# A new order of steps for a linear-attention and gated-convolution kernel, with the last norm factor spread through DRAM

## The chip, the cores and the metric

The kernel runs on one core of one Trainium2 chip. The metric is the device time of one execution in microseconds; the smaller, the better. Times of single steps come from one profiled execution of the kernel before, and are microseconds from the start of its span.

## The reference

Eight batches, each of 576 positions and eight heads of 64. For each head, `kv` is the sum over positions of the outer products of keys and values; the queries times `kv` are normalised by their root mean square over the 64 columns and scaled by `g_norm`. The heads side by side are the 512 columns of `x` of a gated feed-forward layer with a depthwise convolution over three positions in its gate.

```python
kv = np.einsum('bhsd,bhse->bhde', k, v)
out = np.einsum('bhsd,bhde->bhse', q, kv)
rms = np.sqrt(np.mean(out * out, axis=-1, keepdims=True) + 1e-06)
x = (out / rms * g_norm)                 # (B, S, H * D) after a transpose
...
h = np.maximum(x @ w_in, 0.0)            # (B, S, 1024)
conv_out = sum of conv_w[k] * h shifted by k - 1, for k in 0, 1, 2
gate = 1.0 / (1.0 + np.exp(-conv_out))
return (h * gate @ w_out)                # (B, S, 512), float32
```

## The kernel before, in words

The kernel is a list of steps, `ORDER`, run from left to right. Each token is a step: its name, its arguments (most begin with the batch, `b`), and after `@` the buffer that it writes: a PSUM bank for steps of TensorE, a slot of a ring in SBUF for the others. At the end the program chains the instructions of every engine in the order of the list, so each engine does its own steps in exactly this order. A step waits for the steps that make its inputs, and for the last readers of the bank or slot that it takes over.

The steps, by engine:

- Loads on GpSimd's queue: `Lq`, `Lk`, `Lv` (a batch's queries, keys and values, cast to bf16), `Li`, `Lo` (the weights).
- TensorE: `fi` (matmuls of zeros at the start), `qt` (transposes of q), `kv` and `kz` (keys by values), `ot` and `ox` (queries by `kv`), `on` and `oq` (sums of squares, as a product with ones: `on` by full 128x128 matmuls, `oq` by 64x64 ones), `ss` (the same for two batches at once in a compact form, 8 rows in each group of 32), `sp` (the compact norm factor spread over 64 partitions a head, by a matmul with a 0/1 matrix), `hk`, `hs`, `hm` (a 128-column tile of `x @ w_in`; in two parts, for half the positions, for all of them), `cv` (the convolution by matmuls, for four tiles of batch 0), `om` (a 128-row tile of the output; `om.p.m.0.4` and `om.p.m.4.4` are its first and second half over the 1024 columns of `h`), `oh` (a tile in two halves of columns).
- VectorE: `qd`, `kvd`, `ed`, `dh` (evictions of q's transposes, of `kv`, of an output tile, of half of one), `mo` and `mu` (`x`, as output times `g_norm` times factor, one `scalar_tensor_tensor`), `sl` (the compact factor split into three bf16 parts, four instructions), `ta` (the two outer taps of the convolution for one tile of `h`, two instructions), `aa` and `ab` (their sum, then the middle tap), `mg` (`h` times the gate).
- ScalarE: `qa`, `kva`, `ea`, `eh` (the same evictions), `sq` (squares), `oc` (the output copied to fp32), `nl` and `ln` (the factor by a reciprocal square root), `rp`, `rh`, `re` (relu), `sg` and `sc` (sigmoid). A change between root and sigmoid loads a table.
- SP's queue: `st` and `sh` (stores of output rows), `tq` (q transposed by DMA, batches 6 and 7), `kx` (`kv` with its halves of partitions exchanged).

Batches go in pairs that share a buffer `h`. Batches 0 to 3 take the norm factor directly (`on` or `oq`, `nl`, `mo`). Batches 4 and 5, and 6 and 7, take it compactly: `sq` and `oc` of all parts, then `ss`, one `ln` for the pair, `sl`, and for each part (two of heads, `u`, by two of positions, `s`) an `sp` into two banks and a `mu` that reads it from there. `ln.6`, `sl.6`, `sp.6.*`, `sp.7.*`, `mu.6.*` and `mu.7.*` are the last pair's. In batches 6 and 7 a part has 320 positions (`s` = 0) or 256.

The two steps at the centre of the change are these:

```python
@op
def sp(b, u, s, b0):
    ps = T["sp", b, u, s] = bank2()[:, :, :width(b, s)]
    ...
        nc.tensor.matmul(ps[:, tt, :], spread[rows, ...], T["w", b0][rows, :width(b, s)], ...)
@op
def mu(b, u, s):
    nc.vector.scalar_tensor_tensor(
        x_part(b, u, s), T["o32", b, u, s], g_sb, T["sp", b, u, s], op0=AL.mult, op1=AL.mult)
```

The lines of the profile that matter here: L732 `om`, L757 `oh`, L628 `hs`, L658 `hk`, L613 `hm`, L593 `sp`, L566 `ss`, L599 `mu`, L556 `mo`, L581 to L584 `sl`, L681 and L682 `ta`, L687 `aa`, L692 `ab`, L722 `mg`, L743 `ed`, L738 `ea`, L698 `sg`, L640 `rh`, L545 `nl`, L574 `ln`, L416 `kva`, L414 `kvd`, L227 the load of a table, L748 `st`.

Of the kernel before, what the change touches and what calls it, by code (L numbers as in the profile page):

```python
# [54 lines left out]
AL = mybir.AluOpType  # L55
# [4 lines left out]
pre@0,1 af cad.q.0.0@0 cad.v.0.0@0 fi.10.512@0 qt.0.0.0@2 qd.0.0.0@0 gt.k.1.0 Li.0.4 fi.9.512@0 ct@0 Lq.1.0.2@1  # L60
Lk.1.0.2@0 Lv.1.0.2@1 Li.4.4 ps pg fi.4.512@1 cad.k.1.0@1 caa.v.1.0 caa.k.0.0 kv.0.0.1@4 kva.0.0.1@0 ot.0.0.0@6 pc
cad.v.3.0 cad.k.2.0 fi.2.512@0 cad.k.3.0 caa.q.1.0 qt.0.1.0@2 qd.0.1.0@1 sq.0.0.0@0 oq.0.0.0@4 fi.2.512@0 dg.1
caa.v.2.0 kv.0.1.1@0 fi.2.512@2 nl.0.0.0@0 kva.0.1.1 ot.0.1.0@4 sq.0.1.0@1 cad.q.0.1 qt.0.0.1@2 qa.0.0.1 fi.2.512@0
oq.0.1.0@0 nl.0.1.0@1 mo.0.0.0@0 cad.q.1.1 qt.0.1.1@6 qd.0.1.1 mo.0.1.0 ot.0.0.1@2 sq.0.0.1@2 ot.0.1.1@6 fi.1.512@0
sq.0.1.1@3 oq.0.0.1@0 nl.0.0.1@2 fi.1.512@4 fi.1.512@4 hk.0.1.0.0@4 hk.0.1.0.1 rp.1.0@0 on.0.1.1@0 nl.0.1.1@3
hk.0.2.0.0@5 hk.0.2.0.1 rp.2.0 dg.3 mo.0.0.1 dg.2 hk.0.3.0.0@4 hk.0.3.0.1 hk.0.0.0.0@2 hk.0.0.0.1 rp.0.0 hk.0.0.1.0@3
rp.3.0 hk.0.1.1.0@5 hk.0.3.1.0@0 mo.0.1.1 hk.0.3.1.1 rp.3.1 hk.0.1.1.1 rp.1.1 hk.0.0.1.1 rp.0.1 dg.0 hk.0.2.1.0@1
hk.0.2.1.1 qt.1.0.0@6 kv.1.0.1@4 rp.2.1 cv.0.2@2 sc.0.2@0 cv.0.3@0 qd.1.0.0@2 kvd.1.0.1@1 ot.1.0.1@6 sc.0.3 pl
sq.1.0.1@4 cv.0.1@4 cv.0.0@2 Lq.1.2.2 Lk.1.2.2 Lv.1.2.2 sc.0.1@1 fi.2.512@0 qt.1.1.0@0 qd.1.1.0@3 mg.0.1.1 Lo.0.8
sc.0.0 mg.0.1.0 oq.1.0.1@4 nl.1.0.1@4 mo.1.0.1@1 fi.1.512@2 hk.0.5.1.0@2 hk.0.5.0.0@3 hk.0.5.0.1 rp.5.0 hk.0.5.1.1  # L70
rp.5.1 ta.0.1.5@0 hk.0.4.1.0@0 hk.0.4.1.1 rp.4.1 hk.0.7.0.0@1 hk.0.7.0.1 kv.1.1.1@4 kvd.1.1.1 rp.7.0 ot.1.0.0@2
sq.1.0.0@5 hk.0.7.1.0@6 hk.0.7.1.1 rp.7.1 ta.0.1.7@1 ot.1.1.1@0 sq.1.1.1@6 oq.1.0.0@4 nl.1.0.0@5 mo.1.0.0 hk.0.4.0.0@6
hk.0.4.0.1 rp.4.0 hk.0.6.1.0@7 hk.0.6.1.1 rp.6.1 oq.1.1.1@4 nl.1.1.1@6 mo.1.1.1 hk.0.6.0.0@6 Lq.2.0.4@2 hk.0.6.0.1
rp.6.0 ta.0.1.4 hk.1.6.1.0@7 ta.0.1.6 hk.1.0.1.0@2 ot.1.1.0@4 sq.1.1.0@7 aa.0.1.2 hk.1.1.1.0@3 hk.1.2.1.0@6 hk.1.6.1.1
rh.1.6.1 hk.1.1.1.1 rh.1.1.1 on.1.1.0@0 nl.1.1.0@7 mo.1.1.0 hk.1.2.1.1 hk.1.5.1.0@7 hk.1.5.1.1 rh.1.5.1 rh.1.2.1
hk.1.3.1.0@3 hk.1.3.1.1 rh.1.3.1 hk.1.0.1.1 rh.1.0.1 ab.0.1.2 sg.0.1.5 sg.0.1.4 qt.2.1.0@0 qt.2.0.0@6 hk.1.5.0.0@3
hk.1.5.0.1 rh.1.5.0 qd.2.0.0@4 hk.1.0.0.0@2 hk.1.4.1.0@4 hk.1.4.1.1 hk.1.0.0.1 hk.1.1.0.0@5 hk.1.6.0.0@6 hk.1.1.0.1
hk.1.2.0.0@7 hk.1.2.0.1 rh.1.2.0 rh.1.1.0 rh.1.0.0 hk.1.6.0.1 rh.1.6.0 aa.0.1.3 qd.2.1.0@0 ab.0.1.3 sg.0.1.7 sg.0.1.6
hk.1.7.0.0@0 mg.0.1.2 hk.1.7.1.0@1 hk.1.7.1.1 rh.1.7.1 hk.1.7.0.1 rh.1.7.0 ta.1.1.1@0 ta.1.1.0 Lk.2.0.4@1 Lv.2.0.4@0
Lq.3.0.4@0 Lk.3.0.4@0 Lv.3.0.4@1 Lq.4.0.4@1 aa.1.1.0 hk.1.4.0.0@3 om.0.1.0.4@2 rh.1.4.1 hk.1.4.0.1 rh.1.4.0  # L80
om.0.2.0.4@5 kv.2.0.2@6 mg.0.1.3 om.0.1.4.4 ab.1.1.0 sg.1.1.0 sg.1.1.1 kvd.2.0.2@2 ot.2.0.1@0 sq.2.0.1@0 ed.0.1@0
st.0.1 qt.3.1.0@6 qd.3.1.0@1 Lk.4.0.4@1 Lv.4.0.4@0 Lq.5.0.4@2 om.0.2.4.4 on.2.0.1@2 qt.3.0.0@6 qd.3.0.0@2 nl.2.0.1@8
mo.2.0.1@2 om.0.3.0.4@4 ea.0.2@1 ot.2.1.1@6 ot.2.1.0@2 mg.1.1.0 om.0.3.4.4 ed.0.3@2 sq.2.1.0@1 sq.2.1.1@2 on.2.1.0@0
nl.2.1.0@9 mo.2.1.0 om.0.0.0.4@5 hk.1.3.0.0@4 on.2.1.1@0 st.0.2 nl.2.1.1@0 mo.2.1.1 om.0.0.4.4 ed.0.0@3 ot.2.0.0@2
# [54 lines left out]
def kernel(  # L139
# [685 lines left out]
```

## Time and profile before

| | us |
|---|---|
| timed, median of 3 runs (lowest to highest) | 177.59 (177.56 to 177.61) |
| profiled execution: its span | 175.6 |
| TensorE busy | 167.9 |
| VectorE busy | 149.5 |
| ScalarE busy | 148.9 |
| GpSimd busy | 22.2 |

For the profiled execution only the span, from the first to the last instruction, is given; the timed runs are others, and their median is 1.99 us longer than this span. A row of the groups reads: line, engine, operation, what is written from what, shapes, count, then the busy time in us and the mean of one in ns, then the idle time of the engine just ahead of them and what ended it. A row of the chain or of a timeline begins with its start and its length in us. The granted TensorE clock is 1.00 in every stretch.

### The profile page before, as it was taken

How to read it: one execution, taken by the hardware profiler on the slowest of the kernel's cores; microseconds unless marked ns; L12 is line 12 of the kernel's file. 1: busy time of each engine (PE TensorE's matmuls, PEld its weight loads, DVE VectorE, ACT ScalarE, POOL GpSimd, SP SyncE). 2: the span in 40 equal slices, each digit the busy share in tenths (PEclk: the TensorE clock that was granted, in tenths of full speed). 3: DMA queues.
4: the chain of work that ended last, by engine and by line, in shares of the span. 5: the costliest groups of instructions: out<-in, count | busy, mean ns of one | idle time of the engine just before them, and what ended most of it. 6: DMA issues, size and time to landing. Idle time of an engine off the chain costs nothing.

```text
span 175.6 us, 5070 instructions
## 1 busy us (share of the span) xinstructions
PE 167.9 (96%) x2097; PEld 100.0 (57%) x2114; DVE 149.5 (85%) x290; ACT 148.9 (85%) x268; POOL 22.2 (13%) x35
## 2 busy tenths in 40 slices
PE   7979999999999999999999999999999999999992
PEld 2334766676447677644467764444877744444451
DVE  2796638899688899999999998989999999999950
ACT  2368899999978999999999998999999967676721
POOL 3094512200603013030000000000000000000000
PEclk9999999999999999999999999999999999999999
DMA  5999999999999999999999050330310003064486
GB/s 159 392 323 207 207 207 207 208 208 209 207 241 230 227 207 207 170 182 197 258 181 161 14 134 0 119 123 0 119 63 0 0 0 116 13 239 175 179 304 237
DMA packets 25911, 29.11 MB, mean 166 GB/s; under 512 B 6036, under 2 KB 20384, under 8 KB 25888
## 3 DMA queue, kind: packets, MB, share of 16 engines
q0 software_dynamic: 13296, 14.50, 49.2%
q1 hardware_dynamic: 12048, 13.11, 26.2%
q10 hardware_dynamic: 544, 1.18, 1.7%
q8 instruction: 16, 0.26, 0.6%
q14 instruction: 7, 0.06, 0.1%
HBM read 32.52 MB, written 9.44 MB: 239 GB/s over the span
## 4 chain that ended last, share of the span: by engine, by line
PE 76%; DVE 12%; ACT 5%; DMA 3%; issue 3%; ACTq 0%; DVEq 0%
PE banks L732 32%; PE banks L628 14%; PE banks L613 9%; PE banks L658 4%; DMA stg<-in_v_dram 3%; PE banks L460 3%; DVE h L722 2%; PE banks L708 2%; ACT taps L698 2%; PE banks L402 2%; PE banks L593 2%; PE banks L433 1%; PE banks L528 1%; DVE taps L681 1%; PE banks L286 1%
## 5 line engine op out<-in xcount | busy, mean ns | idle before, releaser
L732 PE MATMUL banks<-w_out_sb,h 128*128 128x512 bf16 x267 | 62.8, 379 | 1.2 <-issue 0.6
L698 ACT ACTIVATE taps<-taps,cw 128x576 bf16<-128x576 bf16 (+1 forms) x44 | 40.6, 958 | 5.7 <-DVE taps L692 5.5
L732 PEld LDWEIGHTS <-h 128*128 128x128 bf16 x280 | 26.2, 98 | 30.0 <-issue 1.1
L628 PE MATMUL banks<-x,w_in_sb 128*128 128x288 bf16 (+2 forms) x256 | 34.2, 286 | 0.0
L640 ACT ACTIVATE h<-banks 128x288 bf16<-128x288 f32 (+2 forms) x80 | 29.5, 460 | 0.3 <-PE banks L658 0.2
L628 PEld LDWEIGHTS <-w_in_sb 128*128 128x128 bf16 x256 | 24.4, 98 | 7.8 <-issue 0.8
L722 DVE TENSOR_TENSOR h<-h,taps 128x1152 bf16<-128x1152 bf16 (+1 forms) x24 | 22.8, 952 | 1.2 <-ACT taps L698 1.2
L687 DVE TENSOR_TENSOR taps<-taps 128x1152 bf16<-128x1152 bf16 (+1 forms) x22 | 21.5, 978 | 0.5
L509 ACT ACTIVATE sq<-banks 128x576 bf16<-128x576 f32 (+2 forms) x32 | 20.8, 691 | 1.1 <-PE banks L460 1.1
L692 DVE TENSOR_TENSOR taps<-taps,h 128x1152 bf16<-128x1152 bf16 (+1 forms) x22 | 21.4, 972 | 0.3
L681 DVE TENSOR_SCALAR taps<-h,cw 128x576 bf16<-128x576 bf16 (+1 forms) x44 | 18.7, 424 | 0.6 <-ACT h L665 0.5
L682 DVE TENSOR_SCALAR taps<-h,cw 128x576 bf16<-128x576 bf16 (+1 forms) x44 | 18.4, 418 | 0.0
L738 ACT ACTIVATE row<-banks 128x512 f32<-128x512 f32 x23 | 13.5, 597 | 5.7 <-PE banks L732 4.2
L658 PE MATMUL banks<-x,w_in_sb 128*128 128x288 bf16 (+2 forms) x128 | 17.7, 286 | 0.1
L613 PE MATMUL banks<-x,w_in_sb 128*128 128x288 bf16 x128 | 16.9, 286 | 0.0
L556 DVE SCALAR_TENSOR_TENSOR x<-banks,cw,rs 128x576 bf16<-128x576 f32 (+2 forms) x16 | 13.0, 816 | 3.9 <-ACT rs L545 3.6
L658 PEld LDWEIGHTS <-w_in_sb 128*128 128x128 bf16 x128 | 12.0, 98 | 4.4 <-issue 0.5
L227 ACT ACT_TABLE_LOAD x10 | 12.8, 1283 | 2.0 <-issue 1.8
L613 PEld LDWEIGHTS <-w_in_sb 128*128 128x128 bf16 x128 | 12.3, 98 | 3.7 <-issue 0.2
L443 DVE COPY qT<-banks 128x1152 bf16<-128x1152 bf16 (+2 forms) x13 | 8.8, 681 | 5.7 <-PE banks L433 5.7
L545 ACT ACTIVATE rs<-banks,eps_sb 128x576 f32<-128x576 f32 (+2 forms) x16 | 11.8, 740 | 1.1 <-PE banks L528 1.1
L599 DVE SCALAR_TENSOR_TENSOR x<-o,cw,banks 128x576 bf16<-128x576 f32 (+2 forms) x16 | 12.1, 810 | 0.7 <-PE banks L593 0.5
(89 smaller groups left out, 162.9 us busy)
## 6 DMA issues: line engine op xcount, KB each, us to landing
out_dram<-row SPq DMA_DIRECT2D x35, 256.0 KB, 2.3
q_sb<-in_q_dram POOLq DMA_DIRECT2D x6, 576.0 KB, 17.9
k_sb<-in_k_dram POOLq DMA_DIRECT2D x6, 576.0 KB, 14.5
v_sb<-in_v_dram POOLq DMA_DIRECT2D x6, 576.0 KB, 17.9
stg<-in_v_dram ACTq DMA_DIRECT2D x2, 576.0 KB, 6.2
stg<-in_k_dram SPq DMA_DIRECT2D x4, 288.0 KB, 6.9
w_in_sb<-in_moe_w_in_dram POOLq DMA_DIRECT2D x2, 512.0 KB, 9.9
w_out_sb<-in_moe_w_out_dram POOLq DMA_DIRECT2D x1, 1024.0 KB, 15.5
```

The lines of the kernel that those rows point to most:

```text
L509: nc.scalar.activation(T["sq", b, u, s], T["o", b, u, s], AX.Square)
L613: nc.tensor.matmul(ps[:, s, :HS], w_in_sb[:, t, f * P:(f + 1) * P], T["x", b][:, t, c0:c1], start=(t == 0), stop=(t == NT - 1))
L628: nc.tensor.matmul(ps, w_in_sb[:, t, f * P:(f + 1) * P], T["x", b][:, t, c0:c1], start=(t == 0), stop=(t == NT - 1))
L640: nc.scalar.activation(h, fr, AX.Relu)
L658: nc.tensor.matmul(T[at], w_in_sb[:, t, f * P:(f + 1) * P], T["x", b][:, t, c0:c1], start=(t == 0), stop=(t == NT - 1))
L681: nc.vector.tensor_scalar_mul(tap[:, 0, f % 2, :n, 8:8 + S], h[:, f], cw[:, f:f + 1])
L682: nc.vector.tensor_scalar_mul(tap[:, 1, f % 2, :n, :S], h[:, f], cw[:, 2 * NF + f:2 * NF + f + 1])
L687: nc.vector.tensor_add(tap[:, 1, :, :n, :S], tap[:, 0, :, :n, 7:7 + S], tap[:, 1, :, :n, 1:1 + S])
L692: nc.vector.tensor_add(y, y, span(b, n)[:, 2 * j:2 * j + 2])
L698: nc.scalar.activation(y, y, AX.Sigmoid, scale=cw[:, NF + f:NF + f + 1])
L722: nc.vector.tensor_mul(h, h, tap_of(b, j)[:, 1, :, :n, :S])
L732: nc.tensor.matmul(T["om", p, m], h[:, f, m * P:(m + 1) * P], w_out_sb[:, f, :], start=(f == 0), stop=(f == NF - 1))
```

## The change

1. The whole list is new. Nearly all steps are the same and stand in another order, with other banks and slots. Their numbers differ as follows: `kvd.2`, `kvd.3` become `kva` (ScalarE); `ea.0.4`, `ea.1.0`, `ea.1.2`, `ea.1.4`, `ea.1.8` become `ed` (VectorE); `ed.2.8`, `ed.3.2`, `ed.3.7` become `ea`; `eh.3.8.0` becomes `dh`; `oq.1.0.0` and `oq.1.1.1` become `on`, and `on.2.0.1` becomes `oq`.
2. For batches 6 and 7, `sl.6` and the eight `sp` go. In their place `dw.6` stores the compact factor, 128 x 320 in fp32, to DRAM by SP's queue, and eight `df` fetch it for one part each, by two DMAs of SP's queue, each of which spreads one row over 64 partitions. The fetched tiles lie in slots of the rings of q, k and v, which are free by then. `mu` then reads its factor from SBUF.
3. Some steps are written more generally (`pair` gives one bank for a narrow `on`), and steps that this list does not use are added (`ff`, `ad`).

The new steps, and the changes that the list uses:

```diff
+    dram = pool("dram", 1, space=bass.MemoryType.DRAM)
...
+    def pair(n):
+        if 2 * n <= 512:
+            return bank()[:, :2 * n].rearrange("p (e n) -> p e n", e=2)
+        return bank2()[:, :, :n]
...
     def on(b, u, s):
-        ps = T["on", b, u, s] = bank2()[:, :, :c1 - c0]
+        ps = T["on", b, u, s] = pair(c1 - c0)
...
+    def dw(b0):
+        T["rd", b0] = dram.tile([P, GW], FP32, name="rd")
+        nc.sync.dma_start(out=T["rd", b0], in_=T["rs", b0])
+
+    @op
+    def df(b, u, s, b0):
+        w, c = width(b, s), 2 * (b - b0) + s
+        to = T["sp", b, u, s] = ring("qkv"[(4 * (b - b0) + 2 * u + s) % 3], [P, 2, 320], FP32, "spread")[:, :, :w]
+        fr = T["rd", b0].rearrange("(t c i) w -> c i t w", t=NT, i=2)[c, :, 2 * u:2 * u + 2, :w]
+        for i in range(2):
+            nc.sync.dma_start(out=to[half(i)], in_=fr[i].unsqueeze(0).to_broadcast([D, 2, w]))
```

The list around the last pair's factor, as it was:

```text
... ox.7.0.0@0 oc.7.0.0@8 ox.6.0.1@6 ... mg.2.2.3 om.1.6.4.4 om.1.0.4.4 ...
om.1.1.0.4@4 om.1.1.4.4 ss.6.6.2@5 ss.7.6.2 ln.6@0 ... om.1.4.0.4@0 om.1.4.4.4 ... om.1.7.4.4 ...
sl.6@1 sp.6.1.1.6@6 mu.6.1.1@0 sp.6.0.1.6@4 mu.6.0.1 sp.7.0.0.6@2 mu.7.0.0@2 ... om.1.5.0.4@0 om.1.5.4.4
sp.7.1.0.6@6 mu.7.1.0 sp.7.0.1.6@4 sp.7.1.1.6@2 om.1.3.0.4@1 om.1.3.4.4 ... hs.7.6.0@6 rh.7.6.0@1 mu.7.1.1 mu.7.0.1
...
sp.6.0.0.6@2 mu.6.0.0 sp.6.1.0.6@4 mu.6.1.0 ... aa.4.2.1 ab.4.2.1 ... sg.4.2.2 ... sg.4.2.3 ...
```

and as it is:

```text
... ox.7.0.0@0 ox.6.0.1@2 ... mg.2.2.3 om.1.0.4.4 om.1.6.4.4 kx.7@1 ta.4.2.5@1 ed.1.0@0 ta.4.2.4 ox.7.1.0@0 ta.4.2.6
ox.7.1.1@2 ox.7.0.1@4 om.1.2.4.4 ea.1.6@1 om.1.8.0.4@7 om.1.8.4.4 ed.1.2@2 aa.4.2.2 ... ed.1.8@3 ss.6.6.2@4 sq.7.1.1@6
sq.7.1.0@7 ss.7.6.2 ln.6@0 om.1.4.0.4@5 om.1.4.4.4 ab.4.2.2 aa.4.2.3 sg.4.2.4 hm.4.0@6 om.1.1.0.4@4 om.1.1.4.4
sg.4.2.5 ed.1.4@4 om.1.7.0.4@5 st.1.0 st.1.2 om.1.7.4.4 oc.7.1.1@6 re.4.0 oc.7.1.0@7 st.1.6 dw.6 st.1.8 ab.4.2.3
df.7.0.0.6@0 om.1.5.0.4@2 om.1.5.4.4 mg.4.2.2 om.1.3.0.4@0 om.1.3.4.4 sg.4.2.7 ta.4.2.1@1 ea.1.1@0 ta.4.2.0 ea.1.7@1
aa.4.2.0 mu.7.0.0@0 ea.1.5@2 df.7.1.0.6@0 hm.4.3@2 sg.4.2.6 mu.7.1.0 ea.1.3@3 ab.4.2.0 st.1.4 df.6.1.1.6@1 hs.7.6.0@0
hs.7.4.0@1 hs.7.7.0@4 hs.7.5.0@5 mu.6.1.1@1 re.4.3 df.6.0.1.6@1 mu.6.0.1 mg.4.2.3 rh.7.6.0@1 sg.4.2.1 sg.4.2.0
rh.7.7.0 df.6.0.0.6@2 hm.4.2@2 ... df.6.1.0.6@0 hs.6.0.1@4 ... st.1.1 st.1.5 st.1.7 hs.6.6.1@1 df.7.0.1.6@1 st.1.3
rh.7.2.0 df.7.1.1.6@0 mu.7.0.1 aa.4.2.1 mu.7.1.1 ab.4.2.1 rh.6.6.1 mg.4.2.0 hs.7.2.1@0 rh.7.2.1 hs.7.1.0@2 sg.4.2.3
sg.4.2.2 hs.6.3.0@1 rh.6.3.0 ... hs.7.3.0@1 hs.7.3.1@0 ...
```

Ahead of the table load of batch 1's last sigmoids the old list has `nl.3.1.0@5 ... rh.3.6.1 ... sg.1.1.5 sg.1.1.4 ... mg.1.1.2`, the new one `nl.3.1.0@1 ... sg.1.1.4 ... sg.1.1.5 ...`, with `rh.3.6.1` and `mg.1.1.2` behind them.

More of the change, by code (lines that the diff above doesn't have):

```diff
@@ L65 @@
[L65 to L74, printed above, removed]
@@ L80 @@
[L80 to L84, printed above, removed]
@@ L286, in fi, with ff @@
             nc.tensor.matmul(ps[:, :w], zero[:, :P], zero[:, :w], start=True, stop=True)
+    @op
+    def ff(n, w):
+        ps, z = bank(), zero.bitcast(FP32)
+        for _ in range(n):
+            nc.tensor.matmul(ps[:, :w], z[:, :P], z[:, :w], start=True, stop=True)
     @op
@@ L408, in kvc @@
     def kvc(eng, b, u0, n):
-        if u0 == 0:
+        if ("kvb", b) not in T:
             T["kvb", b] = ring("kvb", [P, 2, 2 * D], BF16, "kvb")
@@ L437, in qc @@
     def qc(eng, b, u, s):
-        if s == 0:
+        if ("qT", b, u) not in T:
             T["qT", b, u] = ring("qT", [P, 2, S], BF16, "qT")
@@ L532, in oq @@
         c0, c1 = cols(b, s)
-        ps = T["on", b, u, s] = bank2()[:, :, :c1 - c0]
+        ps = T["on", b, u, s] = pair(c1 - c0)
         for tt in range(2):
@@ L689, in ab, with ad, y_of @@
     @op
+    def ad(b, n, j):
+        tap = tap_of(b, j)
+        T["y", b, j] = tap[:, 0, :, :n, 7:7 + S]
+        nc.gpsimd.dma_start(out=T["y", b, j], in_=tap[:, 1, :, :n, 1:1 + S], accum_op=AL.add)
+    def y_of(b, n, j):
+        if ("y", b, j) not in T:
+            T["y", b, j] = tap_of(b, j)[:, 1, :, :n, :S]
+        return T["y", b, j]
+    @op
     def ab(b, n, j):
-        y = tap_of(b, j)[:, 1, :, :n, :S]
+        y = y_of(b, n, j)
         nc.vector.tensor_add(y, y, span(b, n)[:, 2 * j:2 * j + 2])
```

149 lines of the change are left out of this document (87 added, 62 removed).

## The prediction

> **What bounds the kernel now.** I read the page first, then the busy time by stretch of 5 us, then the chain of work that ended last, then the rows of single steps. The page's first part:
>
> ```profile
> span 175.6 us, 5070 instructions
> PE 167.9 (96%) x2097; PEld 100.0 (57%) x2114; DVE 149.5 (85%) x290; ACT 148.9 (85%) x268; POOL 22.2 (13%) x35
> ```
>
> TensorE looks like the bound, but the two 85% are averages over a thin start and a thin end. By stretch (span, then PE, PEld, DVE, ACT, POOL, granted clock, DMA share, GB/s):
>
> ```profile
> 50.00:55.00 5.00, 5.00 (x109) 2.91 (x108) 3.46 (x6) 3.56 (x8) 1.48 (x2) 1.00 1.18 240
> 95.00:100.00 5.00, 5.00 (x114) 3.98 (x113) 4.97 (x7) 5.00 (x9) 0.00 (x0) 1.00 0.35 97
> 105.00:110.00 5.00, 4.84 (x33) 2.41 (x32) 4.29 (x8) 4.51 (x8) 0.00 (x0) 1.00 0.00 0
> ```
>
> Up to 60 us VectorE and ScalarE have idle time; around 100 us all three engines are full. VectorE alone, from `mg.1.1.2` to the end of the last `mg`:
>
> ```profile
> 66.51:166.65 100.14, 96.74 (x156) 1.00 0.54 115
> ```
>
> And all that it waited for in that stretch (us in total, times, longest):
>
> ```profile
> DVE h L722 <- ACT taps L698: 1.2, 3, 0.7
> DVE x L599 <- PE banks L593: 0.5, 1, 0.5
> DVE hi L581 <- ACT rs L574: 0.3, 1, 0.3
> DVE kvb L414 <- PE banks L479: 0.2, 1, 0.2
> ```
>
> So VectorE is busy 96.74 of 100.14 us. Of the 2.2 us of waits some 0.2 ended with the first `mg` itself, and only 2.0 lie inside; the other 1.4 are short bubbles between dependent steps. TensorE and VectorE are bounds of nearly the same height, and a step taken from one alone buys little. The chain, at the places that the change touches (start, length, what):
>
> ```profile
> 62.80 0.63 ACT rs L545
> 63.43 0.30 ACT h L640
> 63.74 1.28 ACT L227
> 65.04 1.45 ACT taps L698 x2
> 66.51 0.76 DVE h L722
> ...
> 118.22 0.34 PE banks L593 x4
> ...
> 120.86 0.28 PE banks L593 x2
> 121.15 1.83 PE banks L732 x8
> ...
> 129.74 0.25 PE banks L593 x4
> 129.98 11.11 PE banks L628 x88
> ...
> 141.35 10.74 PE banks L732 x49
> 152.15 10.74 PE banks L732 x49
> 162.94 7.50 PE banks L732 x34
> 170.44 1.76 PE banks L757 x16
> ```
>
> From 121 us to the end, 170.44 + 1.76 = 172.2, TensorE works without a gap; the rest of the span is the last eviction and its store. The span is 175.6 and the timed median 177.59, so 2.0 us lie around the span; I keep these 2.0 and the 3.4 behind TensorE's end, and forecast the shift of TensorE's end.
>
> **What TensorE gets.** The eight `sp` of batches 6 and 7 go (L593, 16 matmuls). Their place is 118.22 to 121.15, 2.93 us, in which one output tile of 8 matmuls ran too (1.83 in the row at 121.15), so 1.10 us are spread and waiting for it; the third group is 0.25. In all 1.35 us. Nothing is added on TensorE: `fi`, `hs`, `hm`, `om` keep their numbers, and in batches 1 and 2 two `oq` become `on` and one `on` an `oq`, short groups far ahead of the place that I find to decide; I cost them at nothing. If TensorE were the only bound, the end would move by −1.35.
>
> **What VectorE gets.** The rows (mean ns stand ahead of the last bar):
>
> ```profile
> L743 DVE COPY row<-banks 128x512 f32<-128x512 f32 x12 | 8.2, 687 | 1.6 <-PE banks L732 1.6
> L599 DVE SCALAR_TENSOR_TENSOR x<-o,cw,banks 128x640 bf16<-128x640 f32 x4 | 3.4, 877 | 0.0
> L599 DVE SCALAR_TENSOR_TENSOR x<-o,cw,banks 128x512 bf16<-128x512 f32 x4 | 2.8, 744 | 0.5 <-PE banks L593 0.5
> L582 DVE SCALAR_TENSOR_TENSOR rs<-hi,na,rs 128x320 f32<-128x320 bf16 x2 | 1.1, 552 | 0.1
> L581 DVE CAST hi<-rs 128x320 bf16<-128x320 f32 x2 | 0.7, 328 | 0.4 <-ACT rs L574 0.3
> ```
>
> And three evictions in a row, from the timeline (start, length):
>
> ```profile
> 166.57 2.00 DVE L743 COPY row<-banks 128x512 f32<-128x512 f32 x3
> ```
>
> `sl.6` goes: two casts and two products, 2 x 0.328 + 2 x 0.552 = 1.76 us. But the new list gives evictions of output rows to VectorE just here: `ed.0.4`, `ed.1.0`, `ed.1.2`, `ed.1.4`, `ed.1.8` were `ea` on ScalarE. Three in a row took 2.00, so five cost 3.3 us. The three that VectorE loses (`ed.2.8`, `ed.3.2`, `ed.3.7`) lie behind the place that I find to decide. The two `kvd` that become `kva` lie ahead of it, where VectorE waits anyway.
>
> The eight `mu` now read the factor from SBUF rather than from a bank. No row shows this very operation. The nearest are the same instruction with one operand in a bank, (877 − 744) / 128 = 1.04 ns an element and so 744 − 532 = 212 ns fixed, and with all in SBUF (L582), 552 − 333 = 219 ns fixed. I take no difference; a fixed part as low as that of the copy from a bank (687 − 532 = 155 ns) would save 0.06 each. [...]
>
> **The fetch.** `dw.6` stores the 128x320 factor to DRAM and each `df` fetches it with two DMAs, all on SP's queue:
>
> ```profile
> out_dram<-row SPq DMA_DIRECT2D x35, 256.0 KB, 2.3
> stq<-in_q_dram SPq DMA_DIRECT2D x2, 320.0 KB, 6.5
> ```
>
> Three issues on SP, from the timeline:
>
> ```profile
> 170.33 1.30 SPq L748 DMA_DIRECT2D out_dram<-row  x3
> ```
>
> A store of 256 KB lands 2.3 us after its issue, and an issue takes 1.30 / 3 = 0.43. The fetch sends the 160 KB of one `dw` and some 164 KB per DMA. From `ln.6` to the second fetched tile: 2.3 for `dw`, three issues, 2.3 for the last DMA, 5.9 us. In the list TensorE has five output tiles (5 x 1.83 = 9.2 us) and two `hm` between `ss.7.6.2` and the first `hs` of batch 7, and VectorE eight other steps ahead of `mu.7.0.0`. The loads are over by then (the stretch at 105 us has a DMA share of 0.00). So I cost the fetch at nothing. The upper bound is the landing time in a full queue, 6.5: then 6.5 + 1.3 + 6.5 = 14.3 plus half a microsecond of `ln`, against 9.2 and two `hm` of 8 matmuls at 11.11 / 88, 11.2 together: 3.6 late. The sixteen fetches hold SP for 16 x 0.43 = 6.9 us, and `st.1.4`, `st.1.1`, `st.1.5`, `st.1.7`, `st.1.3` stand among or behind them; their row buffers are asked for again only by pair 2's evictions some 20 us later.
>
> **The sum.** The new list has a place that the old one had not. `hs.7.3.0@1` needs the bank that `rh.6.3.0` empties, and `rh.6.3.0` stands on ScalarE behind `sg.4.2.3` and `sg.4.2.2`, which wait for VectorE's `ab.4.2.1`. The rows for it, of before, from the timelines of VectorE and ScalarE and from the groups:
>
> ```profile
> 135.03 1.36 DVE L692 TENSOR_TENSOR taps<-taps,h 128x2304 bf16<-128x2304 bf16 x1
> ```
>
> ```profile
> 137.03 2.42 ACT L698 ACTIVATE taps<-taps,cw 128x1152 bf16<-128x1152 bf16 x2
> ```
>
> ```profile
> L640 ACT ACTIVATE h<-banks 128x320 bf16<-128x320 f32 x16 | 7.2, 504 | 0.0
> ```
>
> The 135.03 is `ab.4.2.1`, ending at 136.4. VectorE's work from 66.51 up to it is the same in both lists but for the terms above. Its start moves by −0.3, as the relu at 63.43 no longer stands ahead of the table load; the two `kva` fall into ScalarE's idle 1.4 us of the stretch at 50. Then −1.76 for `sl.6`, +3.3 for five `ed`, and −2.0 if every wait of the stretch goes (the third, for `sp`, goes with it, and the five `ed` fill the others). 136.4 − 0.3 − 1.8 + 3.3 − 2.0 = 135.6. Two sigmoids, 2.4, a relu, 0.5, and 0.1 between engines: `hs.7.3.0` starts at 138.6. Behind it the new list still has 34 halves of output tiles, 6 `hs` and 2 `oh`. The old one ran the same 34 from 141.1 to 170.4, 29.3 us; 24 matmuls at 11.11 / 88 are 3.0; the `oh` 1.8. TensorE ends at 172.7, 0.5 later than the 172.2 of before, though it had 1.35 less to do: without the wait it would stand at `hs.7.3.0` near 172.2 − 1.35 − 34.1 = 136.8. Forecast 177.59 + 0.5 = 178.1.
>
> **Rivals.** First, TensorE alone decides: sigmoids and relus come in time, because VectorE packs tighter than I add up (the 1.4 us of short bubbles may shrink too) or ScalarE reaches the two sigmoids with more lead. For it: TensorE is 96% busy and the chain is TensorE from 121 us on. Against it: VectorE's 96.74 of 100.14. It decides if `ab.4.2.1` ends by 133.8, and gives 177.59 − 1.35 = 176.2. Second, the waits of VectorE do not go but take other forms, as `ed` now waits for output tiles at four places: 2.0 more, 180.1. Third, the fetch lands as in a full queue: 3.6 late, some 181.7 at the least; against it the empty DMA engines. Fourth, the products get shorter by 0.06 each: 0.5 less, 177.6, no change that can be measured (about 0.2%, 0.36 us, is what a measurement of this kernel can tell from no change); the row of L582 speaks against it.
>
> **How the numbers follow.** Forecast 0.50 (177.3 to 179.0), TensorE alone 0.26, VectorE's waits return 0.13, short products 0.08, late fetch 0.03. Faster by over 0.2%: nearly all of the second, 0.25, and 0.02 of the short products. Same: 0.06 of these, 0.08 from the low part of the forecast and 0.01 of TensorE alone, 0.15. Slower: the rest, 0.58. The range goes from TensorE alone, 176.2, to the returned waits, 180.1, and leaves out the late fetch and the outer parts of these two, under 2 in 10; the forecast's own range is 177.3 to 179.0.
>
> **What would show it.** Right: no L593 after 91 us; VectorE without waits of over 0.3 us from 66 to 135 us and busy for over 97% of it; a gap of one to two microseconds in TensorE's `hs`, spread over waits for relus, near 128 and 138 us; the fetched tiles landed some 3 us ahead of their `mu`; a `mu` of 640 columns still at 0.88. Wrong: TensorE without gaps from 121 us to the end and an end near 170.8 (TensorE alone); waits of `mu` for a DMA (late fetch); `ed` waiting for TensorE near 110 us (returned waits); TensorE waiting for loads ahead of 100 us, for which I found no ground.

## The result: some 1.5% slower, by two late fetches

The changed kernel took 180.06 us (median of 4 runs, 179.55 to 181.70), the kernel before 177.57 in the same session: ratio 1.0156, 95% interval 1.0121 to 1.0192. The profiled execution is the longest of the four, 181.7 us with a span of 179.9; the other spans are 177.8 to 178.6. In all the runs below one execution, of e8_copies, fell into a second, slower state, and its time is left out.

The page of the changed kernel, its first part and the granted clock in 40 slices:

```profile
span 179.9 us, 5075 instructions
PE 170.1 (95%) x2096; PEld 100.5 (56%) x2096; DVE 147.7 (82%) x287; ACT 149.2 (83%) x267; POOL 22.3 (12%) x35
...
PEclk9999999999999999999999999999997899999998
```

VectorE is busy 1.8 us less than before. TensorE's busy time grew by 2.2 us although it has fewer matmuls to do; the clock line shows a dip in the slices from 135 to 144 us. The waits of VectorE point at the cause (us in total, times, longest):

```profile
DVE x L631 <- DMA spread<-rd: 2.9, 4, 1.3
```

The row counts four waits of `mu` for a fetched tile: 0.21, 0.19, 1.30 and 1.20 us. The last two, in VectorE's timeline:

```profile
131.20 0.51 DVE L714 TENSOR_SCALAR taps<-h,cw 128x1152 bf16<-128x1152 bf16 x1
133.01 0.75 DVE L631 SCALAR_TENSOR_TENSOR x<-o,cw,spread 128x512 bf16<-128x512 f32 x1 [1.30 <-DMA spread<-rd]
133.68 1.35 DVE L719 TENSOR_TENSOR taps<-taps 128x2304 bf16<-128x2304 bf16 x1
136.23 0.75 DVE L631 SCALAR_TENSOR_TENSOR x<-o,cw,spread 128x512 bf16<-128x512 f32 x1 [1.20 <-DMA spread<-rd]
136.90 1.35 DVE L735 TENSOR_TENSOR taps<-taps,h 128x2304 bf16<-128x2304 bf16 x1
```

The rows at 133.01 and 136.23 are `mu.7.0.1` and `mu.7.1.1`, the one at 136.90 is `ab.4.2.1`. TensorE, whose next `hs` reads what `mu.7.1.1` writes, stands for 2.53 us:

```profile
127.19 7.31 PE L660 MATMUL banks<-x,w_in_sb 128*128 128x256 bf16 x58
137.04 7.39 PE L660 MATMUL banks<-x,w_in_sb 128*128 128x256 bf16 x46 [2.53 <-DVE x L631]
```

Why the tiles came so late is in the timeline of SP's queue (a row merges neighbours; L603 is `dw`, L611 `df`, L793 stores of output rows):

```profile
113.93 0.33 SPq L603 DMA_DIRECT2D rd<-rs  x1
114.34 1.15 SPq L793 DMA_DIRECT2D out_dram<-row  x1
116.49 2.61 SPq L611 DMA_DIRECT2D spread<-rd  x4
119.20 0.53 SPq L793 DMA_DIRECT2D out_dram<-row  x1
119.84 5.19 SPq L611 DMA_DIRECT2D spread<-rd  x8
125.13 1.53 SPq L793 DMA_DIRECT2D out_dram<-row  x3
126.77 1.98 SPq L611 DMA_DIRECT2D spread<-rd  x2
128.85 0.53 SPq L793 DMA_DIRECT2D out_dram<-row  x1
129.90 1.23 SPq L611 DMA_DIRECT2D spread<-rd  x2
```

and in the DMA issues (KB each, median us from issue to landing):

```profile
spread<-rd SPq DMA_DIRECT2D x8, 160.0 KB, 4.5
spread<-rd SPq DMA_DIRECT2D x8, 128.0 KB, 5.0
rd<-rs SPq DMA_DIRECT2D x1, 160.0 KB, 2.5
```

From 116.5 to 131.1 us SP does little but issue. Twelve of the sixteen fetches are issued by 125.0. Then come three stores (`st.1.1`, `st.1.5`, `st.1.7`), the two fetches of `df.7.0.1`, one more store (`st.1.3`) and the two fetches of `df.7.1.1`. These last four are issued at 126.8, 127.9, 129.9 and 130.5 and land at 132.3, 132.9, 135.8 and 136.1. VectorE was ready for the first of the two tiles at 131.7. The chain of waits goes the same way (start, length, what):

```profile
121.82 4.54 DMA spread<-rd
...
130.54 5.59 DMA spread<-rd
136.23 0.76 DVE x L631
137.04 7.39 PE banks L660 x46
...
175.56 0.89 PE banks L802 x8
```

Before, TensorE carried the chain from 121 us on; now it goes through a fetch up to 136.1, and TensorE ends at 176.45 where it ended at 172.2. Some of that belongs to this execution alone: by stretch (span, PE, PEld, DVE, ACT, POOL, granted clock, DMA share, GB/s)

```profile
130.00:135.00 5.00, 4.51 (x36) 3.27 (x34) 3.70 (x6) 4.54 (x12) 0.00 (x0) 1.00 0.66 161
135.00:140.00 5.00, 2.96 (x15) 1.92 (x15) 3.80 (x7) 2.23 (x4) 0.00 (x0) 0.75 0.01 2
140.00:145.00 5.00, 5.00 (x37) 3.70 (x36) 4.93 (x11) 4.36 (x11) 0.00 (x0) 0.91 0.00 0
```

the clock granted after the gap is 0.75 and then 0.91. 0.25 of the first stretch and 0.09 of the second are 1.7 us; this execution has a mean clock of 0.987, the other three 0.999 to 1.0, and their spans are 1.3 to 2.1 us shorter. The other three have no trace. Without a dip of the clock they are still some 1.7 to 2.5 us slower than e1_early below, which is about the length of the gap; that they have the gap too is inferred from this.

### The profile page after: what moved, and what is told of

Read it like the earlier page. It is cut to its first block, busy times and chain, and to the rows that moved or that the text cites. A ratio compares the mean times of both kernels' runs of the same rounds, so it can differ in the third digit from the quotient of the medians.

```text
span 179.9 us, 5075 instructions
## 1 busy us (share of the span) xinstructions
PE 170.1 (95%) x2096; PEld 100.5 (56%) x2096; DVE 147.7 (82%) x287; ACT 149.2 (83%) x267; POOL 22.3 (12%) x35
## 2 busy tenths in 40 slices
DMA packets 28359, 31.63 MB, mean 176 GB/s; under 512 B 6308, under 2 KB 22832, under 8 KB 28336
## 4 chain that ended last, share of the span: by engine, by line
PE 57%; ACT 19%; DMA 10%; DVE 6%; issue 3%; SPq 3%; ACTq 0%; DVEq 0%
PE banks L777 24%; PE banks L660 8%; PE banks L690 7%; DMA spread<-rd 6%; ACT taps L741 4%; PE banks L645 4%; DVE x L631 3%; ACT sq L523 3%; ACT h L672 3%; DMA stg<-in_v_dram 3%; SPq L611 3%; PE banks L474 3%; ACT h L651 2%; PE banks L294 2%; PE banks L447 2%
## 5 line engine op out<-in xcount | busy, mean ns | idle before, releaser
L777 PE MATMUL banks<-w_out_sb,h 128*128 128x512 bf16 x280 | 64.7, 379 | 0.0
L741 ACT ACTIVATE taps<-taps,cw 128x576 bf16<-128x576 bf16 (+1 forms) x44 | 40.0, 960 | 2.3 <-DVE taps L735 2.2
L660 PE MATMUL banks<-x,w_in_sb 128*128 128x288 bf16 (+2 forms) x256 | 36.2, 295 | 2.7 <-DVE x L631 2.5
L660 PEld LDWEIGHTS <-w_in_sb 128*128 128x128 bf16 x256 | 25.2, 100 | 12.0 <-issue 3.3
L783 ACT ACTIVATE row<-banks 128x512 f32<-128x512 f32 x21 | 12.1, 596 | 7.4 <-PE banks L777 3.9
L690 PE MATMUL banks<-x,w_in_sb 128*128 128x288 bf16 (+2 forms) x128 | 17.7, 286 | 0.0
L645 PEld LDWEIGHTS <-w_in_sb 128*128 128x128 bf16 x128 | 12.3, 98 | 4.9 <-issue 1.1
L690 PEld LDWEIGHTS <-w_in_sb 128*128 128x128 bf16 x128 | 12.1, 98 | 3.9
L788 DVE COPY row<-banks 128x512 f32<-128x512 f32 x14 | 9.5, 682 | 5.0 <-PE banks L777 5.0
L294 PE MATMUL banks<-zero 128*128 128x512 bf16 x37 | 11.4, 432 | 1.2 <-DVE zero L273 1.2
```

The costliest lines, as they stand in the source:

```text
L645: nc.tensor.matmul(ps[:, s, :HS], w_in_sb[:, t, f * P:(f + 1) * P], T["x", b][:, t, c0:c1], start=(t == 0), stop=(t == NT - 1))
L660: nc.tensor.matmul(ps, w_in_sb[:, t, f * P:(f + 1) * P], T["x", b][:, t, c0:c1], start=(t == 0), stop=(t == NT - 1))
L690: nc.tensor.matmul(T[at], w_in_sb[:, t, f * P:(f + 1) * P], T["x", b][:, t, c0:c1], start=(t == 0), stop=(t == NT - 1))
L741: nc.scalar.activation(y, y, AX.Sigmoid, scale=cw[:, NF + f:NF + f + 1])
L777: nc.tensor.matmul(T["om", p, m], h[:, f, m * P:(m + 1) * P], w_out_sb[:, f, :], start=(f == 0), stop=(f == NF - 1))
```

## The experiments

The theory after the trace: the two last fetches are late because they are issued late, behind the other fetches, which are dear to issue (0.60 us each in the median, on SP), and five stores in one queue. The rivals: the new list itself sets the end (the working of the prediction), or the DMA engines are slow with these fetches, whatever the order.

| run | what it is | us | ratio to before, 95% interval |
|---|---|---|---|
| e1_early | last two fetches ahead of the four stores | 177.90 | 1.0014 (1.0005 to 1.0023) |
| e2_two_queues | every second fetch DMA on GpSimd's queue | 178.15 | 1.0025 (1.0009 to 1.0041) |
| e4_fetch_alone | the old list with the fetch | 188.90 | 1.0633 (1.0618 to 1.0647) |
| e6_list_alone | the new list with the old spread | 186.45 | 1.0501 (1.0484 to 1.0519) |
| e6b_list_alone | the same, `sp` better placed | 183.98 | 1.0359 (1.0343 to 1.0375) |
| e5_own_rows | each partition fetches a row of its own (not the factor that it needs) | 177.04 | 0.9969 (0.9959 to 0.9979) |
| e7_one_dma | one DMA for each part | 220.31 | 1.2416 (1.2381 to 1.2451) |
| e8_copies | the same from four copies | 183.34 | 1.0328 (1.0307 to 1.0349) |
| e9_early_copies | the same in the order of e1_early | 181.05 | 1.0196 (1.0181 to 1.0212) |
| e12_merged | two DMAs, packets of 2,560 bytes | 178.36 | 1.0045 (1.0031 to 1.0058) |
| e10_copies | the same from four copies | 180.12 | 1.0128 (1.0101 to 1.0155) |
| e11_early_copies | e10_copies in the order of e1_early | 178.58 | 1.0053 (1.0041 to 1.0066) |
| e13_early_merged | e12_merged in the order of e1_early | 177.91 | 1.0017 (1.0008 to 1.0027) |
| e14_relu_first | e13, one relu and one store moved | 177.73 | 1.0007 (0.9998 to 1.0016) |

**The order in the queue.** Two tokens move:

```diff
-... df.6.1.0.6@0 hs.6.0.1@4 ... st.1.1 st.1.5 st.1.7 hs.6.6.1@1 df.7.0.1.6@1 st.1.3 rh.7.2.0 df.7.1.1.6@0 mu.7.0.1 ...
+... df.6.1.0.6@0 df.7.0.1.6@1 df.7.1.1.6@0 hs.6.0.1@4 ... st.1.1 st.1.5 st.1.7 hs.6.6.1@1 st.1.3 rh.7.2.0 mu.7.0.1 ...
```

> The fetches of the parts 7.0.1 and 7.1.1 are issued right behind that of 6.1.0, ahead of the four stores st.1.1, st.1.5, st.1.7 and st.1.3; nothing else moves. Late fetch (my theory after the trace): the two last tiles land by about 131, ahead of the 131.7 at which VectorE is ready for them, both waits of 1.3 and 1.2 us go, ab.4.2.1 ends at about 135.6 and not 138.2, TensorE's gap of 2.5 us at 134.5 goes and with it the dip of the clock: 177.3 to 177.8, no change against before that can be measured, or a little faster. Rival, the order of the list holds VectorE (the working of the prediction): another gap of 1 to 2 us appears near 138, 178.1 or more. Rival, the DMA engines are slow with these fetches whatever stands around them: the last tiles still land 5 to 6 us behind their issue, the waits stay near 1 us, 179 or more.

177.90 us, just above the 177.3 to 177.8 expected: 2.2 of the 2.5 us are gone. The last four fetch DMAs are issued 1.6 to 3.5 us earlier. They take 4.4 to 4.9 us to land, like most of the other twelve, where behind the stores they took 5.0 to 5.9; so they land at 129.5 to 131.8, in time. VectorE's timeline and TensorE's:

```profile
131.65 0.74 DVE L630 SCALAR_TENSOR_TENSOR x<-o,cw,spread 128x512 bf16<-128x512 f32 x1
132.31 1.35 DVE L718 TENSOR_TENSOR taps<-taps 128x2304 bf16<-128x2304 bf16 x1
133.58 0.74 DVE L630 SCALAR_TENSOR_TENSOR x<-o,cw,spread 128x512 bf16<-128x512 f32 x1
134.25 1.35 DVE L734 TENSOR_TENSOR taps<-taps,h 128x2304 bf16<-128x2304 bf16 x1
```

```profile
127.14 11.00 PE L659 MATMUL banks<-x,w_in_sb 128*128 128x256 bf16 x88 [0.17 <-DVE x L630]
138.45 2.14 PE L659 MATMUL banks<-x,w_in_sb 128*128 128x320 bf16 x16 [0.32 <-ACT h L671]
```

Both waits and the gap of 2.53 us are gone; `ab.4.2.1` ends at 135.60. So the lateness of two fetches, by their place in SP's queue, is what made the change slow; that is shown. The third theory falls: the other twelve DMAs are as slow as before. Of the gap of 1 to 2 us near 138, which the working of the prediction calls for, a wait of 0.32 is left. The time is still 0.25 us above the kernel before.

**Two queues.** The fetch's second half goes to GpSimd:

```diff
-            nc.sync.dma_start(out=to[half(i)], in_=fr[i]...)
+            (nc.sync, nc.gpsimd)[i].dma_start(out=to[half(i)], in_=fr[i]...)
```

> List as in the change; of the two DMAs of each fetch the second is issued on GpSimd's queue, which has nothing else to do by then. If SP's issues (0.6 us each, sixteen of them and six stores in a row) set the landing: SP's share ends some 4 us earlier, the last tiles land near 131, the waits of mu go, 177.3 to 177.8. If the DMA engines set it (same bytes, same packets): landings stay 4 to 6 us behind the issue and the last near 135, 179 to 180.5.

178.15 us, between the two expectations and nearly as good as e1_early. The last tile lands at 132.4 and not at 136.1. But the landing grew (DMA issues):

```profile
spread<-rd POOLq DMA_DIRECT2D x4, 128.0 KB, 6.3
spread<-rd SPq DMA_DIRECT2D x4, 128.0 KB, 6.5
```

against 5.0 in the change. The first fourteen DMAs are now issued at 116.6 to 123.3, one in 0.5 us, and land at 120.8 to 130.0, one in 0.71; in the change SP alone issues one in 0.65. From 121 to 129 us the DMA engines' share is 1.00 to 1.08. I read from this that the fetches now queue in the DMA engines, whose limit is nearly that of one queue's issue.

**The halves of the change alone.** The fetch in the old list:

```diff
-sl.6@1 sp.6.1.1.6@6 mu.6.1.1@0 sp.6.0.1.6@4 mu.6.0.1 ...
+dw.6 df.6.1.1.6@1 mu.6.1.1@0 df.6.0.1.6@1 mu.6.0.1 ...
```

> The list of before, with dw and df standing in the places of sl and sp and nothing else changed: the spread through DRAM alone. TensorE has 1.35 us less to do and VectorE 1.76 less. Late fetch: in that list dw stands directly ahead of the first mu. ln.6 ends at 116.3, the factor lands in DRAM at 118.7, the first tile near 122.5 and the sixth near 130.5; VectorE waits some 4 us for the first mu and 1.3 us for each further one, TensorE idles 5 to 7 us between its output tiles and the hs of batch 7: 182 to 185. Rival, the fetch is cheap and the new list is what costs: 176 to 178.

188.90 us, above the expected 182 to 185. The waits of VectorE:

```profile
DVE x L630 <- DMA spread<-rd: 12.1, 5, 6.4
```

The first wait is 6.4 us where some 4 were expected, and the clock fell with it: from 120 to 135 us it is 0.70 in the mean. And the new list with the old spread, where each `sp` needs two free banks near its `mu`:

> The new list with the spread of before: sl.6 in the place of dw.6, and eight sp in free banks near their mu in the place of the fetches. No fetch, so no late fetch. Against e1_early TensorE has 1.35 us more to do and VectorE 1.76. If the two are bounds of nearly the same height, as the prediction had it, ab.4.2.1 ends near 137 and the end moves by 1.4 to 1.8 against e1_early: 179.2 to 179.8. Rival, the new list is as good or better with the old spread, and all that was lost is the fetch: 177.0 to 178.0.

186.45 us, far above the 179.2 to 179.8 expected; VectorE waits 6.8 us in all for four `sp`, 3.4 the longest. The `sp` stood behind `hs` steps that had waits of their own. The second try:

```diff
-... ea.1.3@3 ab.4.2.0 ... df.6.1.1.6@1 hs.7.6.0@0 ... re.4.3 ... mu.6.0.1 ... df.6.0.0.6@2 ... hs.6.4.1@6 ... mu.6.0.0 ...
+... ea.1.3@3 re.4.3 ab.4.2.0 ... sp.6.1.1.6@6 sp.6.0.1.6@2 hs.7.6.0@0 ... mu.6.0.1 sp.6.0.0.6@6 ... hs.6.4.1@4 ... mu.6.0.0 sp.6.1.0.6@6 ...
```

> As e6_list_alone, where the sp stood too late in TensorE's order (VectorE waited 2.6 and 3.4 us for two of them): here they stand ahead of the hs of their neighbours, one hs takes another bank, and re.4.3 comes two steps earlier. If TensorE and VectorE are bounds of nearly the same height, the end moves by 1.4 to 1.8 against e1_early, for 1.35 us more on TensorE and 1.76 on VectorE: 179.2 to 179.8, and 180.5 where an sp still waits for a bank. Rival, the new list needs no fetch to be as good: 177.0 to 178.0.

183.98 us, again above the expected 179.2 to 180.5, and still with waits for `sp` (L624):

```profile
DVE x L630 <- PE banks L624: 5.3, 3, 3.2
```

This can't price the order by itself, since the places of the `sp` are mine and two of them were still bad. It suggests something else: the new list keeps the banks full of `hs`, and an `sp` needs a pair of banks and a turn in TensorE's order. The fetch needs neither. So what the fetch buys here may be freedom from banks and from TensorE's order more than TensorE's time; no run with well placed `sp` tests this.

**Why a landing takes 4.6 us.** Each partition fetches another piece of the stored factor, in the list of the change:

```diff
+        rows = T["rd", b0].rearrange("(p t) w -> p t w", t=2)[:, :, :w]
         for i in range(2):
-            nc.sync.dma_start(out=to[half(i)], in_=fr[i].unsqueeze(0).to_broadcast([D, 2, w]))
+            nc.sync.dma_start(out=to[half(i)], in_=rows)
```

> List as in the change; each fetch DMA reads 64 different pieces of the stored factor, one for each partition, where the change reads one row 64 times; bytes, packets and queues are the same, the values are those of other rows. If many reads of one row are what makes the landing slow: landing falls from 4.6 to some 2.5 us behind the issue, the last tile lands near 133 and the waits of mu are under 0.5 us, 177.5 to 178.5. If issue and bytes set it: landing 4 to 5 us as before, 179.5 to 180.5.

```profile
spread<-rd SPq DMA_DIRECT2D x8, 160.0 KB, 3.2
spread<-rd SPq DMA_DIRECT2D x8, 128.0 KB, 3.4
```

The DMAs of 128 KB, with the same 1,024-byte packets, land in 3.4 us and not in 5.0, and the issues stay at 0.5 to 0.6 us, a few at 0.8. (Those of 160 KB also got larger packets, since their two columns are neighbours here: the whole run moved 27,847 packets and not 28,359, 64 fewer for each of these eight.) So reading one row 64 times costs more than a microsecond of landing. The time, 177.04, is below the expected 177.5 to 178.5 and lower than that of any other run. Its trace shows no shorter TensorE path than e13's and e14's below, but that trace is of its slowest execution (177.45, the others 176.97 to 177.19). The tiles hold rows other than those that `mu` needs, so I use the landings and leave the time open.

**One DMA for each part.** The factor is stored so that a part's two columns are neighbours, and one DMA fetches a part:

```diff
+        fr = T["rd", b0][2 * c:2 * c + 2].rearrange("i n t w -> (i n) (t w)")[:, 2 * u * GW:(2 * u + 2) * GW]
+        nc.sync.dma_start(
+            out=to.rearrange("p t w -> p (t w)"), in_=fr.unsqueeze(1).to_broadcast([2 * REP, D // REP, 2 * GW]))
```

> List as in the change. The factor lies in DRAM so that the two columns of a part are neighbours, and each fetch is one DMA of 128 packets of 2,560 bytes where the change has two (of 128 packets of 1,280 or 1,024 bytes); the store of the factor is four small DMAs, two on SP and two on GpSimd. If the number of issues on SP sets the landing: eight issues of 0.6 us fewer, the last tile lands near 132, the waits of mu go, 177.3 to 178.0. If an issue costs by its packets or bytes: 1.2 us each, landings as in the change, 179.5 to 180.5. If the DMA engines are slow at reading one row many times: landing 6 us or more behind the issue, but all issues 4 us earlier, 178 to 179.

220.31 us, far outside all that was expected. A tile came every 6 to 8 us (VectorE's `mu` start that far apart), and a stretch between two of them shows why:

```profile
132.00:136.00 4.00, 2.79 (x11) 1.57 (x11) 2.15 (x2) 2.03 (x3) 0.00 (x0) 0.50 0.13 51
```

The DMA engines' mean share is 0.13 at 51 GB/s, as much as two engines of sixteen would give (2/16 = 0.125). The source pattern begins with a dimension of 2. That this leading dimension keeps the share so low is my reading of the row; the runs below bear on it. With four copies (REP = 4) the source begins with a dimension of 8:

> As e7_one_dma, but the factor is stored in four copies, and each fetch reads each copy of a row 16 times instead of one row 64 times. If many reads of one row make the landing slow, the landing is 1 to 2 us shorter than in e7_one_dma and the waits of mu are gone: 177.0 to 177.6. If not, it is as e7_one_dma, or 0.5 us later for the larger store.

> The list of e1_early (the last two fetches ahead of the four stores) with the four copies and one DMA for each fetch. No mu waits any more, also not the 0.3 and 0.2 us near 125 and 126 that e1_early still has: ab.4.2.1 ends near 135.3, TensorE has no gap in its hs: 176.8 to 177.4, 0.1 to 0.4% faster than before. Rival, the order of VectorE's steps holds hs.7.3.0 as in e1_early: 177.7 to 178.0.

183.34 and 181.05 us. The first was off by 6 us and the second by 4. A stretch of e8_copies in which little but fetches moves shows a DMA share of 0.53 at 204 GB/s, about half (8/16 = 0.5):

```profile
131.00:134.00 3.00, 2.93 (x25) 2.24 (x24) 2.71 (x5) 2.66 (x7) 0.00 (x0) 1.00 0.53 204
```

In both of these the copies and the leading dimension changed together, so they say nothing about the repeated row. The same layout with two DMAs for each part, whose source begins with the repetition of 64:

```diff
+            in_=fr.unsqueeze(0).to_broadcast([D // REP, REP, 2 * GW]))   # for each half i; REP = 1 in e12, 4 in e10 and e11
```

> List as in the change, two DMAs for each part as in the change, each spread over its 64 partitions first, so that all 16 DMA engines should share it; the factor lies in DRAM so that a part's two columns are neighbours: 64 packets of 2,560 bytes for each DMA where the change has 128 of 1,280 or 1,024. e7_one_dma differs from it only in that one DMA begins with a dimension of 2. If that dimension is what cost e7_one_dma 40 us (its DMA engines were busy to 0.13, two of sixteen), this one is within 1.5 us of the change: 178.0 to 180.5. If packets of this size or many reads of one row cost it, it is above 190. Landing some 4 us behind the issue, if the number of packets counts; as in the change (4.6), if the repeated row does.

```profile
spread<-rd SPq DMA_DIRECT2D x16, 160.0 KB, 4.2
```

178.36 us, in the list of the change. The DMA engines' share from 118 to 134 us is 0.80 at 247 GB/s, where e7_one_dma has 0.17 at 63. So the leading dimension cost e7_one_dma its 40 us. (e12_merged also has two DMAs for a part where e7_one_dma has one; but e8_copies, with one and a leading dimension of 8, already lost most of the 40.) The landing is 4.2 us with half as many packets for each part (27,287 in the whole run, 28,359 in the change), and the late waits fall to 0.36 us.

> As e12_merged with the factor stored in four copies, each row read 16 times and not 64 times. If the repeated row is what makes the landing long (4.6 us in the change, 3.4 with rows of its own for each partition): 3.4 to 3.8 us here, but the store of four copies lands 1 us later; 177.3 to 178.5. If not: as e12_merged and some 0.5 later.

```profile
spread<-rd SPq DMA_DIRECT2D x16, 160.0 KB, 3.7
```

Each row read 16 times and not 64: 3.7 us, half a microsecond less, as e5_own_rows had it in direction. In the order of e1_early the same step saves only 0.1: 3.7 in e11_early_copies, 3.8 in e13_early_merged below. The time is 180.12, above the expected. The store of four copies lets the first fetch start 0.8 us later than in e12_merged and the last 1.05, and the last lands in 4.6 us and not in 3.6, so that `mu.7.1.1` waits 1.54 us again; why that landing is longer I can't say.

> e10_copies in the list of e1_early, the last two fetches ahead of the four stores. No mu waits more than 0.3 us: 177.0 to 177.5, like the run with rows of its own, where the landing was short too. If the later store of the copies makes the first mu late instead: 177.8 to 178.5.

178.58 us: the later store eats the shorter landing; `mu.6.0.1` waits 0.68 us.

**What holds the rest.** e13 puts e12's layout into e1's order; e14 lets `sg.4.2.2` stand behind `rh.6.3.0` and `st.1.4` behind all fetches:

```diff
-... hs.7.1.0@2 sg.4.2.3 sg.4.2.2 hs.6.3.0@1 rh.6.3.0 ...
+... hs.7.1.0@2 sg.4.2.3 hs.6.3.0@1 rh.6.3.0 sg.4.2.2 ...
```

> The list of e1_early with the DRAM layout of e12_merged (packets of 2,560 bytes, landing 4.2 and not 4.6 us behind the issue). If what is left of the fetch's lateness is what holds e1_early at 177.9: no wait of mu over 0.2 us, 177.2 to 177.6. If hs.7.3.0 behind its relu holds it: 177.7 to 178.0, with the wait of 0.32 us as it was.

> As e13_early_merged, and sg.4.2.2 stands behind rh.6.3.0 on ScalarE, so that hs.7.3.0 waits for one sigmoid and not for two; st.1.4 goes behind all fetches, which then issue 0.6 us earlier. If the bound that the prediction named (hs.7.3.0 at 138.6) is what holds TensorE's end: the wait of 0.32 us at 138.5 goes and the end comes 0.3 to 0.6 earlier than in e13_early_merged, 176.7 to 177.3. If not: within 0.2 of e13_early_merged.

177.91 and 177.73 us. In e13 no wait of a `mu` for a tile is listed any more, and the time stays that of e1_early: what remained of the fetch's lateness cost nothing that can be measured. Nor does the second expectation fit, since the wait of 0.32 us is gone too. TensorE's row in e13, where e1_early had two:

```profile
126.88 13.14 PE L667 MATMUL banks<-x,w_in_sb 128*128 128x256 bf16 x104
```

So e13 to e14 doesn't test that wait. (The traces of e1 and e13 are both of executions of 177.63 us, faster than their medians.) e14 is 0.18 below e13, less than the 0.3 to 0.6 expected, and cannot be told from the kernel before; whether the sigmoid or the store made the 0.18 is open. Of the versions that fetch the right rows none beats the kernel before.

## Why the prediction was right or wrong, step by step

**The fetch is the step that failed.** The prediction costed it at nothing by looking at the first two tiles. These were in time: `mu.7.0.0` and `mu.7.1.0` ran without a wait at 122.07 and 123.08. But they were so by little: the second tile landed at 122.96, 9.0 us behind `ln.6` and not 5.9. And the prediction did not follow the other six. Three numbers were off. An issue took 0.6 us (0.66 for the first), not 0.43, the price of a store. A landing took 4.6, not 2.3, again that of a store; of the gap, e5_own_rows gives more than 1 us to the repeated row. And sixteen such DMAs with five stores fill one queue from 116.5 to 131.1. The prediction did see that stores "stand among or behind them", but asked only who waits for the stores, not which fetch waits behind them. The argument against the late fetch, empty DMA engines, was wrong in itself: in the stretch of the fetches, 118 to 134 us, the engines' share is

```profile
118.00:134.00 16.00, 15.87 (x110) 10.47 (x109) 14.13 (x20) 14.82 (x29) 0.00 (x0) 1.00 0.89 229
```

0.89, where the kernel before has 0.14 in the same stretch. They were empty before because the fetches were not there. The rival had the mechanism but put it at the first tiles (3.6 late); it came at the last two (1.3 and 1.2 on VectorE, 2.53 on TensorE), and its chance of 0.03 was far too low.

**VectorE's walk came out, in part by luck.** With the fetch in time (e1_early) `ab.4.2.1` ends at 135.60 (predicted 135.6), `hs.7.3.0` is started at 138.45 behind its relu (138.6), and the time is 177.90 (178.1). Two terms hold: `mg.1.1.2` starts at 66.10 (predicted 66.2), and the five `ed` take 0.68 to 0.69 each, 3.4 in all (3.3). The term for the waits does not. The prediction let all 2.0 us of them go, but in e1_early 1.7 are still listed between 66.10 and 135.60, 0.4 of them for fetched tiles. What made up for it is not in the sum: the short bubbles fell from 1.0 to 0.3, and VectorE's busy time, in which overlapping instructions count once, grew by only 0.6 where the sum added 1.5. Errors of some 1.7 us one way and 1.6 the other cancel; that is luck. VectorE is busy for 66.8 of the 68.8 us from 66.2 to 135, 97%, as foretold.

That the relu ahead of `hs.7.3.0` decides the time is not borne out. The prediction had TensorE ready for this step at 136.8; in e1_early it was ready at 138.1 and waited 0.32. In e13's trace `ab.4.2.1` ends 0.7 earlier, this wait is gone, and TensorE ends 0.57 earlier; yet the two traced executions took the same 177.63 us. TensorE's last rows in the chains of e1, e13 and e14:

```profile
171.58 1.05 PE banks L801 x8
171.01 1.05 PE banks L809 x8
171.12 1.05 PE banks L810 x8
```

From TensorE's end to the end of the span these need 3.2, 3.6 and 3.6 us, where the prediction kept 3.4: half a microsecond at TensorE's end can vanish behind it.

**TensorE's 1.35 us were given up elsewhere.** No L625 runs after 91.4, as foreseen. But e14 has no wait of TensorE that the trace lists between 111 us and the end, and still ends at 171.12 + 1.05 = 172.17, where before it was 172.2. So the rival of TensorE alone, 176.2, would have missed too: the prediction took the rest of the order as free for TensorE. Where they went I estimate by counting. From the last `sp` of batches 4 and 5 to the end of `om.1.3.4.4` the kernel before runs 13 `hm` and 18 halves of output tiles in 32.5 us (90.29 to 122.82), e14 12 and 18 in 31.3 (91.55 to 122.86). An `hm` is 8 matmuls of 0.122 us, by the two rows of before below, and a half is 4 of 0.216 (19.02 us for 88 in the chain of the changed kernel). What remains for everything else is 4.3 us before, 1.1 of it for `sp`, and 4.0 in e14, which has no `sp` there: 0.8 lost. Another 0.3 is lost ahead of it, since e14 enters the stretch 1.26 us later with one `hm`, 0.98, less to do. Together that is the 1.1 that the `sp` gave there. The rows of the `hm` (L613 before, L653 in e14):

```profile
90.29 6.05 PE L613 MATMUL banks<-x,w_in_sb 128*128 128x288 bf16 x48
...
97.27 3.11 PE L613 MATMUL banks<-x,w_in_sb 128*128 128x288 bf16 x24
```

```profile
91.55 4.26 PE L653 MATMUL banks<-x,w_in_sb 128*128 128x288 bf16 x32
...
96.11 3.35 PE L653 MATMUL banks<-x,w_in_sb 128*128 128x288 bf16 x24
...
107.37 0.30 PE L514 MATMUL banks<-qT,kvx 64*64 64x256 bf16 x4 [0.21 <-ACT h L659]
```

The group of 24 takes 3.35 us where it took 3.11, and the group of 32 takes 4.26 where the rows of before give 3.11 + 8 x 0.122 = 4.09: 0.4 us in waits too short to be listed. In the last row an `ox` waits 0.21 for a relu. ScalarE carries e14's chain of waits from 96 to 114 us. This is read from the rows; no run isolates it.

**The other rivals.** The products did not get shorter: a `mu` of 640 columns takes 0.88 and one of 512 takes 0.75 as before, so the rows of the same instruction, 212 and 219 ns fixed, were a better guide than the copy's 155, and the 0.5 us that the prediction set aside did not come. Most of VectorE's waits stayed, as told above, but they did not return at the `ed`: these waited 0.2 us in all for TensorE from 66 to 136 us. The time fell into the range, at its upper end, which had been put there for the returned waits and not for what happened.

## What to carry to other kernels

A DMA that replaces a step on an engine is scheduled work: walk its queue to the last transfer, with every store that stands between, and compare each landing with its own reader, not only the first. Price it by a row of the same shape (here many small packets from one row: 0.6 us to issue, 4.6 to land), and count what it does itself to the load of the engines. When the step it replaces had set the order, move both halves together: neither the fetch in the old list (188.9) nor the old spread in the new list (184.0) came near either kernel, in the places that were tried. And a time that comes out as predicted does not make the terms right: redo the sum term by term.

## What the runs showed of the hardware

A fetch whose source pattern began with a dimension of 2 ran at 51 GB/s and a DMA share of 0.13, as much as two engines of sixteen (e7_one_dma), and one with a leading dimension of 8 at 204 GB/s and 0.53 (e8_copies). The same bytes with a leading dimension of 64, in two DMAs for each part, ran at 247 GB/s and 0.80 from 118 to 134 us (e12_merged) and kept the kernel at 178.4 us and not at 220.3. DMAs of 128 KB that read one DRAM row 64 times landed in 5.0 us (the change), against 3.4 for rows of their own with the same packets (e5_own_rows); reading it 16 times and not 64 saved 0.5 in one order of the queue and 0.1 in another. And a gap of 2.53 us on TensorE was followed by a clock of 0.75 and 0.91 in the next two stretches of 5 us; in steps of 1 us it is 0.50 from 138 to 140. The other three executions of the change, with a mean clock of 0.999 to 1.0, had no such drop. Gaps of 1.90 us (e10_copies, a mean clock of 1.0 in that execution) and 1.81 (e8_copies, 1.00 from 122 to 136 us) were not followed by a lower clock.
